# A forward 640-point transform in five full 128-row tables in place of four full ones and 32-row remainders

## The chip, the cores and the metric

The kernel runs on one core of one Trainium2 chip. Its time is device time in microseconds (us) of one execution. Before the change the median of three runs is 203.46 us (203.17 to 204.21). The core has TensorE (matmuls, PE in a profile, its weight loads PEld), VectorE (DVE), ScalarE (ACT), GpSimd (POOL) and SyncE (SP), which here issues all DMAs. Each engine works through its own instructions in order and waits on semaphores for the others.

## The reference

Two branches work on the layernormed input, `x` of 2048 rows and 640 columns, in bfloat16.

```
xn  = layernorm(x)                                   # over the 640 columns
s   = irfft2( rfft2(xn) * (w_r + i w_i) )            # 2048 x 321 spectrum
g   = silu( (gelu(xn @ w_gate) * (xn @ w_up)) @ w_down )   # 640 -> 1536 -> 640
out = x + s * g
```

So there is a feed-forward network (FFN), and beside it a two-dimensional Fourier transform, a product with a spectrum and the way back. The transform is made of matmuls with sine tables that the kernel builds itself.

## The kernel before, in words

The 2048 rows are split as 128 x 16: slab `n1` (0 to 15) holds the 128 rows with the remainder `n1`, and lies as a `[128, 640]` slice of `X`. The FFN runs in four groups `g` of four slabs: per group 24 halves (`ffn_half`: gate or up product of one tile of 128 of the 1536 features, five matmuls of 512 columns) and 12 thirds (`down_third`: eight matmuls of 320 columns each). A gate half ends in a gelu on ScalarE (`ge`), an up half in a product on VectorE (`uT`). Their PSUM banks `psg` and `psu` have two buffers each.

The spectral work is woven between the pieces of the FFN. The order of all engines is written out by hand: `back` is the list of FFN pieces, and `put(s, ...)` hangs an item behind piece `s`. Nothing reorders it afterwards. Pieces 16 to 23 are the last halves of FFN group 0, 24 to 35 its thirds, 36 to 59 the halves of group 1, 60 to 71 its thirds. Since every engine works in that order, an item whose input is late holds back what was put behind it on the same engine.

The forward transform of one slab has these steps:

- `stats`, `root`, `norm`: mean and variance on VectorE, the power -0.5 on GpSimd, the norm in place on VectorE (slabs 4 to 7 on ScalarE).
- `fold_a`, `fold_b`, for a pair of slabs on VectorE: sums and differences of the two halves of the 640 columns (`uvt`), then of mirrored columns. This uses the symmetry of cosines and sines and of even and odd frequencies, and leaves four blocks of 160 values. They are stored as four chunks of 128 and one chunk of 4 x 32.
- `slab_S1`: five matmuls, one per chunk, with the table `Tfwd` of the slab: the transform along the rows. ScalarE copies the result from PSUM (`pz`) to `Zt`, one of four places in `zbuf`.
- `group_D`, for one slab and then five groups of three (`DF`): the transform along the columns with the table `FT`. Each block of 160 is one matmul with 128 rows and one with 32 rows, both 161 columns wide, the second added to the first in PSUM (`d_group`). The two PSUM tiles `pd` are then copied, written to every other element of `zd`, and four DMAs per group bring `zd` to the DRAM scratch `ZDR`.

The PSUM pool `psB` has two buffers, which `pz`, the two `pd` tiles of a group and, outside this stage, other tiles take in turn. So the transform behind a group waits until the group's first `pd` tile has been copied out.

After the last group, `load_B2` reads `ZDR` back as `B`; it is the gate between the forward stage and the second row stage (`s2_in`, first matmuls `px`), the product with the spectrum, and the way back, which uses `d_group` with another table (`FI`). GpSimd also builds the tables `MG` (`mg_build`) and halves the edge columns of the weights (`w_edge`).

Of the kernel before, what the change touches and what calls it, by code (L numbers as in the profile page):

```python
# [14 lines left out]
P = 128  # L15
# [3 lines left out]
LP = 322  # L19
LH = 161  # L20
HD = 160
F = 1536
NT = F // P
NS = 16
# [52 lines left out]
def build(nc, env):  # L77
# [59 lines left out]

    Tinv = consts.tile([P, NS, P], BF16)
    Tfwd = consts.tile([P, NS, P], BF16)
    FT = consts.tile([P, 5, LH], BF16)  # L140
    FI = consts.tile([P, 5, LH], BF16)
    MG = consts.tile([P, 2, 2, 64], BF16)
    N1 = consts.tile([P, 2, P], BF16)
# [6 lines left out]
    def gtile(shape, dt):  # L150
        n = 1
        for k in shape:
            n *= k
        w = n if dt != BF16 else n // 2
        ap = GEN[:, goff[0]:goff[0] + w]
        goff[0] += w
        assert goff[0] <= NH * L // 2
        if dt != INT32:
            ap = ap.bitcast(dt)
        if len(shape) > 1:  # L160
            names = "abcdefg"[:len(shape)]
            ap = ap.rearrange("p (%s) -> p %s" % (" ".join(names), " ".join(names)), **dict(zip(names, shape)))
        return ap
# [58 lines left out]
    make_identity(nc, ident)  # L222
    lint = gtile([LH], INT32)
    nc.gpsimd.iota(lint, pattern=[[1, LH]], base=0, channel_multiplier=0)
    vt = gtile([NS, P], INT32)

    def vt_iota(h):
# [13 lines left out]
    def affine(name, src, a, b):  # L241
        t = c1(name)
        nc.vector.tensor_scalar(out=t, in0=src, scalar1=float(a), scalar2=float(b), op0=ALU.mult, op1=ALU.add)
        return t
# [19 lines left out]
    def times(name, src, k, by):  # L264
        t = c1(name)
        nc.vector.scalar_tensor_tensor(out=t, in0=src, scalar=k, in1=by, op0=ALU.mult, op1=ALU.mult)
        return t
# [8 lines left out]

    def fwd_consts():
        cq = affine("cq", h_f, -320.0, 320.0)
        a_m = affine("a_m", pf, 4.0, 130.0)
        b_2 = affine("b_2", pf, 2.0, 385.0)  # L280
        b_3 = affine("b_3", pf, 2.0, 65.0)
        a_r = affine("a_r", s_f, 4.0, 2.0)
        s21 = affine("s21", s_f, 2.0, 1.0)
        b_r = fma("b_r", times("hs", s21, 1.0, hi_f), 1.0, cq)
        kc.append(cq)
        ab.extend([(a_m, b_0), (a_m, b_1), (a_m, b_2), (a_m, b_3), (a_r, b_r)])

    def inv_consts():
        i_0 = affine("i_0", pf, 4.0, 0.0)
# [46 lines left out]
    ftm = gtile([5, LH], FP32)  # L336

    def ft_v(g):
        nc.scalar.activation(out=fv[:, g, :], in_=lint, func=ACT.Identity, scale=ab[g][0], bias=ab[g][1])

    def ft_phase(t, k):
        v = fv[:, 5 * t:5 * t + 5, :]
        if k == 0:
            nc.gpsimd.tensor_scalar(out=ftm, in0=v, scalar1=1.0 / 1280.0, scalar2=MAGIC, op0=ALU.mult, op1=ALU.add)
        elif k == 1:
            nc.gpsimd.tensor_scalar(out=ftm, in0=ftm, scalar1=MAGIC, scalar2=-1280.0, op0=ALU.subtract, op1=ALU.mult)
        else:
            nc.gpsimd.tensor_tensor(out=v, in0=v, in1=ftm, op=ALU.add)

    def ft_sin(t):  # L350
        nc.scalar.activation(out=(FT, FI)[t], in_=fv[:, 5 * t:5 * t + 5, :], func=ACT.Sin,
                             scale=TWO_PI / 1280.0 * (1.0 - 2e-7))

    mg = {}
# [86 lines left out]
        done.add(("n", n1))  # L441

    uvs = {}

    def fold_a(pair):
        xn = X[:, 2 * pair:2 * pair + 2, :]
        assert ("n", 2 * pair + 1) in done
        uvs[pair] = uvt = work.tile([P, 2, D], BF16, tag="uv", bufs=2, name="uvt")
        nc.vector.tensor_tensor(out=uvt[:, :, 0:320], in0=xn[:, :, 0:320], in1=xn[:, :, 320:640], op=ALU.add)
        nc.vector.tensor_tensor(out=uvt[:, :, 320:640], in0=xn[:, :, 0:320], in1=xn[:, :, 320:640], op=ALU.subtract)  # L450

    def fold_b(pair):
        xf[pair] = f = work.tile([P, 2, D], BF16, tag="xf", bufs=2, name="f")
        s4 = uvs.pop(pair).rearrange("p k (t d) -> p k t d", t=2)
        dm = f[:, :, 0:512].rearrange("p k (g d) -> p k g d", g=4)
        dr = f[:, :, 512:640].rearrange("p k (g d) -> p k g d", g=4)
        for gs, op in ((slice(0, 4, 3), ALU.add), (slice(1, 3), ALU.subtract)):
            nc.vector.tensor_tensor(out=dm[:, :, gs, :], in0=s4[:, :, :, 32:160], in1=s4[:, :, :, 287:159:-1], op=op)
            nc.vector.tensor_tensor(out=dr[:, :, gs, :], in0=s4[:, :, :, 0:32], in1=s4[:, :, :, 319:287:-1], op=op)

    def chunk(f, k, c):
        return f[:, k, c * P:(c + 1) * P]

    def slab_T(n1, eng):
        assert ("n", n1) in done
# [16 lines left out]
    zbuf = fv.rearrange("p g l -> p (g l)").bitcast(BF16)[:, 0:4 * D].rearrange("p (s c k) -> p s c k", s=4, c=5)  # L482

    def slab_S1(n1):
        f = xf[n1 // 2]
        pz = psB.tile([P, 5, P], FP32, tag="b")
        for c in range(5):
            nc.tensor.matmul(pz[:, c, :], lhsT=chunk(f, n1 % 2, c), rhs=Tfwd[:, n1, :], start=True, stop=True)  # L488
        Zt[n1] = zbuf[:, n1 % 4]
        nc.scalar.copy(out=Zt[n1], in_=pz)  # L490

# [13 lines left out]
    DF = [(0, 1)] + [(n0, 3) for n0 in range(1, NS, 3)]  # L505
    DG = [(n0, min(3, NS - n0)) for n0 in range(0, NS, 3)]

    def group_D(i):
        n0, n = DF[i]
        pd = d_group([Zt.pop(n0 + a) for a in range(n)], FT, LH)  # L510
        zd = work.tile([P, 3, 2, LP], BF16, tag="zd", bufs=2, name="zd")[:, 0:n]
        for b in range(2):
            ev = nc.vector.tensor_copy if i in (2, 5) and b == 1 else nc.scalar.copy
            ev(out=zd.rearrange("p a c (m b) -> p a c m b", b=2)[:, :, :, :, b], in_=pd[b])  # L514
        for a in range(2):
            if n == 1:
                nc.sync.dma_start(out=ZDR[a, :, n0].rearrange("c p l -> p c l"), in_=zd[a:P:2, 0, :, 0:L])
            else:
                for c in range(2):
                    nc.sync.dma_start(out=ZDR[a, c, n0:n0 + n].rearrange("n p l -> p n l"),  # L520
                                      in_=zd[a:P:2, :, c, 0:L])

    warm_bank = []

# [308 lines left out]
        put(17 + 2 * k, slab_T, 4 + k, 2)  # L833
    put(17, stats, 8)
    put(19, stats, 9)
    put(23, fold_a, 0)
    for it in ((silu_table,), (tinv_sin, 0), (tinv_sin, 1), (ft_sin, 0)):
        put(23, *it)
    put(24, fold_b, 0)
    put(28, mg_mask)  # L840
    put(25, root, 8, 2)
    put(25, fold_a, 1)
    for q in range(4):
        put(24 + q, tfwd, q)
    put(27, norm, 8)
    put(28, fold_b, 1)
    put(29, stats, 10)
    put(28, ft_sin, 1)
    put(29, mg_sin)
    put(29, mg_build)  # L850
    put(31, norm, 9)
    put(32, stats, 11)
    put(33, root, 10, 2)
    put(34, norm, 10)
    put(35, norm, 11)
    put(38, stats, 12)
    put(41, stats, 13)
    put(41, root, 12, 2)
    put(42, stats, 14)
    put(43, norm, 12)  # L860
    put(44, norm, 13)
    put(44, stats, 15)
    put(45, root, 14, 2)
    put(46, norm, 14)
    put(47, norm, 15)
    F0 = 30
    for i, (n0, n) in enumerate(DF):
        a = F0 if i == 0 else F0 + 5 * i - 3
        for k in range(n):
            put(a + k, slab_S1, n0 + k)  # L870
        put(a + n, group_D, i)
    for pair in range(6):
        b = F0 + 3 * pair + (0 if pair < 4 else 3)
        put(b, fold_a, pair + 2)
        put(b + 1, fold_b, pair + 2)
    z_end = F0 + 26
    for k in range(4):
        put(32 + 3 * k, slab_T, 8 + k, 2)
# [85 lines left out]
```

## Time and profile before

| what | value |
|---|---|
| median of the runs shown | 203.46 us (203.17 to 204.21) |
| the profiled execution | 203.13 us |
| its span, first to last instruction | 201.1 us |
| mean granted TensorE clock | 0.998 |
| TensorE busy, instructions | 194.5 us, 1558 |
| VectorE busy | 128.1 us |
| ScalarE busy | 122.6 us |
| GpSimd busy | 34.0 us |
| forward stage, first transform to the last group's end | 42.6 to 81.4 us |
| first `B` load issued, first `px` matmul | 88.19 us, 92.53 us |

A profile here has a page and answers from the trace. A line of the groups gives line of the kernel, engine, operation, output and inputs by the program's names, shape and count, and then busy us, mean ns of one, and the idle time of the engine before them with what ended it. A timeline line gives start, duration, engine, line and operation, and how many equal instructions are merged. Matmuls overlap and their ends are modelled, so TensorE is read by the distance between starts. The chain of work that ended last is followed back from the last instruction, step by step, to what released it.

### The profile page before, as it was taken

The numbers are of one execution on the slowest core, as the hardware profiler recorded it, in microseconds if no ns is written. First come the engines' busy times: TensorE is split into PE (matmuls) and PEld (weight loads), VectorE is DVE, ScalarE is ACT, GpSimd is POOL, SyncE is SP. The second block draws the span as 40 slices with busy tenths as digits, with TensorE's granted clock in tenths as the row PEclk, the third lists the DMA queues.
The fourth block names the chain that finished last, engine by engine and source line by source line (L and its number), as shares of the span: only waits on it lengthen the run. The fifth ranks groups of instructions, "written<-read, shape, count | busy, mean of one in ns | idle before, by whom it ended". The sixth has DMA issues, their size and how long they took to land.

```text
span 201.1 us, 4180 instructions
## 1 busy us (share of the span) xinstructions
PE 194.5 (97%) x1558; PEld 118.9 (59%) x1573; DVE 128.1 (64%) x339; ACT 122.6 (61%) x209; POOL 34.0 (17%) x61
## 2 busy tenths in 40 slices
PE   7899999999999999999999999999999999999993
PEld 5678854777555555576644333457775555556762
DVE  7786966677398972544566475333258777867672
ACT  2448657966886777414888778325475647476631
POOL 4327779972101100000000000000000000000000
PEclk9999999999999999999999999999999999999999
DMA  6999999656566675139944102379401444224312
GB/s 173 308 301 307 372 341 186 135 144 232 124 173 156 158 276 171 54 97 296 243 134 132 64 34 101 131 179 316 163 0 65 101 115 117 72 91 140 92 62 68
DMA packets 39444, 32.29 MB, mean 161 GB/s; under 512 B 14209, under 2 KB 37377, under 8 KB 39169
## 3 DMA queue, kind: packets, MB, share of 16 engines
q1 hardware_dynamic: 39424, 32.04, 55.9%
q8 instruction: 12, 0.20, 0.4%
q14 instruction: 8, 0.06, 0.1%
HBM read 19.03 MB, written 7.88 MB: 134 GB/s over the span
## 4 chain that ended last, share of the span: by engine, by line
PE 91%; DVE 5%; issue 1%; POOL 1%; ACT 0%
PE psu L727 25%; PE psg L727 25%; PE psg L751 13%; PE psu L751 12%; PE pd L498 5%; PE pz L488 2%; PE pv L644 2%; PE pu L592 2%; PE pd L502 2%; PE px L565 2%; DVE st L182 1%; POOL rst L198 1%; DVE X L204 1%; DVE mva L187 0%; DVE uT L733 0%
## 5 line engine op out<-in xcount | busy, mean ns | idle before, releaser
L727 PE MATMUL psu<-xnT,Wu 128*128 128x512 bf16 (+2 forms) x289 | 61.0, 339 | 0.7 <-issue 0.2
L727 PE MATMUL psg<-xnT,Wg 128*128 128x512 bf16 (+2 forms) x286 | 60.3, 338 | 1.0 <-issue 0.5
L733 DVE TENSOR_TENSOR uT<-psu,ge 128x512 bf16<-128x512 f32 (+2 forms) x59 | 34.3, 584 | 30.1 <-PE psu L727 22.5
L731 ACT ACTIVATE ge<-psg 128x512 bf16<-128x512 f32 (+2 forms) x59 | 30.5, 518 | 27.8 <-PE psg L727 25.9
L751 PEld LDWEIGHTS <-uT 128*128 128x128 bf16 x384 | 36.3, 98 | 14.7 <-issue 0.6
L727 PEld LDWEIGHTS <-Wu 128*128 128x128 bf16 x295 | 26.6, 98 | 23.0 <-issue 2.9
L727 PEld LDWEIGHTS <-Wg 128*128 128x128 bf16 x295 | 26.6, 98 | 21.9 <-issue 1.6
L751 PE MATMUL psg<-Wd,uT 128*128 128x320 bf16 (+1 forms) x192 | 30.2, 303 | 0.0
L751 PE MATMUL psu<-Wd,uT 128*128 128x320 bf16 (+1 forms) x192 | 29.2, 296 | 0.0
L577 DVE TENSOR_TENSOR X<-xs,W 128x972 bf16<-128x972 bf16 (+2 forms) x22 | 13.3, 648 | 10.2 <-ACT xs L573 10.2
L646 ACT CAST W<-pv 128x640 bf16<-128x640 f32 x16 | 11.1, 692 | 5.4 <-PE pv L644 5.4
L182 DVE BATCH_NORM_STATS2 st<-X 128x6 f32<-128x320 bf16 x32 | 14.2, 482 | 0.0
L514 ACT CAST zd<-pd 128x966 bf16<-128x966 f32 (+1 forms) x10 | 10.4, 1100 | 5.3 <-PE pd L502 5.3
L669 ACT ACTIVATE W<-pd 128x960 bf16<-128x960 f32 (+2 forms) x14 | 10.1, 780 | 5.0 <-PE pd L502 4.9
L490 ACT CAST GEN<-pz 128x640 bf16<-128x640 f32 x16 | 11.0, 696 | 3.2 <-PE pz L488 3.2
L598 ACT CAST X<-pu 128x486 bf16<-128x486 f32 (+4 forms) x22 | 12.3, 557 | 0.3
L573 ACT CAST xs<-px 128x972 bf16<-128x972 f32 (+2 forms) x11 | 10.3, 937 | 2.1 <-PE px L565 2.1
L198 POOL TENSOR_TENSOR rst<-ve,mhalf 128x1 f32<-128x1 f32 (+2 forms) x9 | 6.5, 717 | 26.6 <-DVE ve L196 26.6
L675 DVE TENSOR_TENSOR W<-W 128x960 bf16<-128x960 bf16 (+1 forms) x12 | 6.8, 600 | 4.8 <-ACT W L669 4.8
L702 DVE TENSOR_TENSOR Yall<-Yall,G 128x640 bf16<-128x640 bf16 (+3 forms) x18 | 8.1, 450 | 2.1 <-ACT G L756 1.9
L760 DVE SCALAR_TENSOR_TENSOR G<-th,psu 128x320 bf16<-128x320 f32 x8 | 3.9, 488 | 8.2 <-ACT th L759 8.2
L703 DVE TENSOR_TENSOR Yall<-Yall,xt 128x640 bf16<-128x640 bf16 (+3 forms) x18 | 8.2, 455 | 0.6
(138 smaller groups left out, 198.0 us busy)
## 6 DMA issues: line engine op xcount, KB each, us to landing
W<-W SPq DMA_DIRECT2D x4, 642.0 KB, 4.2
xt<-in_A_x_dram SPq DMA_DIRECT2D x8, 320.0 KB, 3.8
ZDR<-zd SPq DMA_DIRECT2D x20, 120.4 KB, 3.2
UDR<-X SPq DMA_DIRECT2D x10, 240.8 KB, 2.5
out_dram<-Yall SPq DMA_DIRECT2D x14, 160.0 KB, 2.1
B<-ZDR SPq DMA_DIRECT2D x8, 240.8 KB, 4.2
W<-UDR SPq DMA_DIRECT2D x4, 481.5 KB, 7.0
X<-in_A_x_dram SPq DMA_DIRECT2D x3, 640.0 KB, 7.1
```

What stands on the lines that cost most here:

```text
L182: nc.vector.bn_stats(out=st[:, k, :], in_=X[:, n1, 320 * k:320 * k + 320])
L490: nc.scalar.copy(out=Zt[n1], in_=pz)
L514: ev(out=zd.rearrange("p a c (m b) -> p a c m b", b=2)[:, :, :, :, b], in_=pd[b])
L573: nc.scalar.copy(out=xs, in_=px[:, :, 0:n * w].rearrange("p k (h l) -> p k h l", l=w))
L577: nc.vector.tensor_tensor(out=pp[-1], in0=xs, in1=WT[:, :, h0:h0 + n, l0:l0 + w], op=ALU.mult)
L598: nc.scalar.copy(out=us[:, :, :, c0:c0 + (w + 1 - m) // 2], in_=pv[:, :, :, m:w:2])
L646: nc.scalar.copy(out=vs, in_=pv)
L669: nc.scalar.activation(out=eo[:, b, :, a0:a1].rearrange("p k a n -> p a k n"), in_=py[b][:, a0:a1], func=ACT.Copy, scale=(2.0 if silu[a0] ...
L727: nc.tensor.matmul(ps, lhsT=WT[:, c, t * P:(t + 1) * P], rhs=xnT[g][:, c, c0:c1_], start=(c == 0), stop=(c == 4))
L731: nc.scalar.activation(out=ges[t], in_=ps, func=ACT.Gelu_apprx_tanh)
L733: nc.vector.tensor_tensor(out=uT[g][:, t, c0:c1_], in0=ps, in1=ges[t], op=ALU.mult)
L751: nc.tensor.matmul(ph, lhsT=uT[g][:, t, j * P:(j + 1) * P], rhs=Wd[:, t, c0:c1_], start=(t == 0), stop=(t == NT - 1))
```

## The change

The frequencies 0 to 320 are split into those divisible by five and the others.

- For the first, only the sum of the five blocks of 128 columns matters. `fold_y` forms it for a pair of slabs in three additions (512, 256 and 256 elements); it is the fifth chunk, 128 values. Pairs 0 and 1 have it on VectorE, pairs 2 to 7 on GpSimd.
- For the others, adding the same block to all five blocks changes nothing, so `fold_x` subtracts one block from the others (two instructions, 768 and 256 elements). `fold_a` and `fold_b` then work on the four blocks left, with two additions or subtractions of 512 elements each, and give four chunks of 128.
- The table `FT` has five parts of 128 columns; sample points are moved by half a step, so that the columns that are always zero need no entry. They are set once by a memset in `zds`, two fixed buffers in place of the pool's.
- `group_D` does five matmuls of 128 rows and 128 columns per slab. The four first chunks go to four PSUM banks, and the fifth to the free end of these banks. The copies to `zd` are one of all groups' 768 elements, two of 384, one of 256 and one of 128; the elements go to strides of two in runs of four or two, and of five. In groups 1 and 5 the second bank pair's copies are VectorE's, before it was in groups 2 and 5.
- The plan of statistics, norms and folds is written anew. Statistics 14 and 15, their norms and the fold of the last pair lie three to four pieces later than before, and `mg_build` eight pieces later.

```diff
-    FT = consts.tile([P, 5, LH], BF16)
+    FT = consts.tile([P, 5, P], BF16)
+    zds = [consts.tile([P, 3, ZW], BF16, name=f"zd{k}") for k in range(2)]
+    for k in range(2):
+        nc.gpsimd.memset(zds[k][:, :, 325:326], 0.0)
...
+    def fold_y(pair, eng):
+        xn = pair_x(pair)
+        y0s[pair] = y = work.tile([P, 2, P], BF16, tag="y0", bufs=3, name="y0")
+        t = ytbuf
+        for out, i0, i1 in ((t, xn[:, :, 0:256], xn[:, :, 256:512]), (y, t[:, :, 0:P], t[:, :, P:256]),
+                            (y, y, xn[:, :, 512:640])):
+            eng.tensor_tensor(out=out, in0=i0, in1=i1, op=ALU.add)
+
+    def fold_x(pair):
+        xn = pair_x(pair)
+        xps[pair] = xp = xpbuf
...
+        ref = blocks(xn)[:, :, 2:8:5, :]
+        nc.vector.tensor_tensor(out=outer(xp), in0=outer(xn),
+                                in1=ref.unsqueeze(1).to_broadcast([P, 3, 2, 2, 64]), op=ALU.subtract)
+        nc.vector.tensor_tensor(out=blocks(xp)[:, :, 6:2:-3, :], in0=blocks(xn)[:, :, 6:2:-3, :], in1=ref,
+                                op=ALU.subtract)
...
     def fold_a(pair):
...
-        nc.vector.tensor_tensor(out=uvt[:, :, 0:320], in0=xn[:, :, 0:320], in1=xn[:, :, 320:640], op=ALU.add)
-        nc.vector.tensor_tensor(out=uvt[:, :, 320:640], in0=xn[:, :, 0:320], in1=xn[:, :, 320:640], op=ALU.subtract)
+        lo, hi = (xp[:, :, o:o + 384].rearrange("p s (t e) -> p s t e", e=192)[:, :, :, 0:P] for o in (0, 320))
+        for k, op in enumerate((ALU.add, ALU.subtract)):
+            nc.vector.tensor_tensor(out=uvt[:, :, 256 * k:256 * k + 256].rearrange("p s (t e) -> p s t e", e=P),
+                                    in0=lo, in1=hi, op=op)
...
     def fold_b(pair):
...
         for gs, op in ((slice(0, 4, 3), ALU.add), (slice(1, 3), ALU.subtract)):
-            nc.vector.tensor_tensor(out=dm[:, :, gs, :], in0=s4[:, :, :, 32:160], in1=s4[:, :, :, 287:159:-1], op=op)
-            nc.vector.tensor_tensor(out=dr[:, :, gs, :], in0=s4[:, :, :, 0:32], in1=s4[:, :, :, 319:287:-1], op=op)
+            nc.vector.tensor_tensor(out=dm[:, :, gs, :], in0=s4[:, :, :, 0:P], in1=s4[:, :, :, 255:127:-1], op=op)
...
+    BY_DVE = (1, 5)
...
     def group_D(i):
         n0, n = DF[i]
-        pd = d_group([Zt.pop(n0 + a) for a in range(n)], FT, LH)
...
+        ps = [psB.tile([P, 2, 512], FP32, tag="b", name=f"pd{b}") for b in range(2)]
+        for a in range(n):
+            z = Zt.pop(n0 + a)
+            for g in range(5):
+                o = ps[g // 2][:, g % 2, a * P:a * P + P] if g < 4 else ps[a // 2][:, a % 2, 384:512]
+                nc.tensor.matmul(o, lhsT=z[:, g, :], rhs=FT[:, g, :], start=True, stop=True)
...
+        ev[0](out=zq[:, :, :, :, 2:10:2], in_=src[0].rearrange("p a c (q r) -> p a c q r", r=4))
+        for h in range(2):
+            ev[1](out=zq[:, :, :, :, 1 + 6 * h:4 + 6 * h:2],
+                  in_=src[1][:, :, :, 64 * h:64 * h + 64].rearrange("p a c (q i) -> p a c q i", i=2))
+        for b in range((n + 1) // 2):
+            m = min(2, n - 2 * b)
+            ev[b](out=y_cols(zd, 2 * b, m), in_=ps[b][:, 0:m, 384:512].rearrange("p a (c m) -> p a c m", c=2))
...
+            (40, (stats, 13), (root, 12, 2)), (41, (fold_a, 4)),
+            (42, (fold_b, 4), (norm, 12)), (43, (norm, 13), (half_stats, 14, 0), (fold_y, 6, gp)),
+            (44, (fold_x, 5), (half_stats, 14, 1)), (45, (fold_a, 5)), (46, (fold_b, 5), (fold_x, 6)),
+            (47, (fold_a, 6)), (48, (fold_b, 6), (half_stats, 15, 0)), (49, (half_stats, 15, 1), (root, 14, 2)),
+            (50, (norm, 14), (norm, 15), (fold_y, 7, gp)), (51, (fold_x, 7)), (52, (fold_a, 7), (fold_b, 7))):
```

## The prediction

> **What bounds the kernel now.** I read the page's busy shares, then the chain that ended last, then the groups by form, and last the timelines of the engines around the forward 640-point stage (42 to 82 us).
>
> ```profile
> span 201.1 us, 4180 instructions
> ...
> PE 194.5 (97%) x1558; PEld 118.9 (59%) x1573; DVE 128.1 (64%) x339; ACT 122.6 (61%) x209; POOL 34.0 (17%) x61
> ...
> PE 91%; DVE 5%; issue 1%; POOL 1%; ACT 0%
> ```
>
> TensorE carries 91% of the chain and idles 6.6 us in all. So a us of matmul removed is a us gained, unless another engine makes TensorE wait; every edit is judged by that. The granted clock is 0.998, with nothing to gain there. The profiled execution took 203.13 us (span 201.1, 2.0 outside), 0.33 below the median of 203.46.
>
> The stage's matmuls, from TensorE's timeline (start, us, line, count):
>
> ```profile
> 49.71 1.02 PE L498 MATMUL pd<-FT,GEN 128*128 128x161 bf16 x12
> 50.67 0.39 PE L502 MATMUL pd<-FT,GEN 32*128 32x161 bf16 x12
> 50.99 0.39 PE L727 MATMUL psg<-xnT,Wg 128*128 128x512 bf16 x1
> ...
> 60.97 0.44 PE L488 MATMUL pz<-Tfwd,f 128*128 128x128 bf16 x5
> 61.25 0.38 PE L727 MATMUL psu<-xnT,Wu 128*128 128x512 bf16 x1
> ```
>
> Ends are modelled, so starts count: a group of three slabs holds TensorE from 49.71 to 50.99, 1.28 us; five 128x128x128 matmuls, each with weights of its own, 0.28 us, or 56 ns each.
>
> Groups by form (busy us, mean ns of one) give the other prices; VectorE's eviction of 966 elements stands there with 1240 ns:
>
> ```profile
> L514 ACT CAST zd<-pd 128x966 bf16<-128x966 f32 x8 | 9.5, 1245 | 4.8 <-PE pd L502 4.8
> ...
> L458 DVE TENSOR_TENSOR f<-uvt 128x512 bf16<-128x512 bf16 x16 | 6.7, 421 | 2.0 <-PE pz L488 2.0
> ...
> L348 POOL TENSOR_TENSOR GEN<-GEN 128x805 f32<-128x805 f32 x2 | 3.2, 1612 | 0.2
> ...
> L514 ACT CAST zd<-pd 128x322 bf16<-128x322 f32 x2 | 0.9, 521 | 0.5 <-PE pd L502 0.5
> ```
>
> **TensorE.** A full group becomes 15 matmuls of the 56 ns kind, 0.84 us for 1.28: 5 x 0.44 = 2.2. The first group (4 + 4 matmuls, 43.95 to 44.51, 0.56) becomes five, 0.28. Group 2 also waited 0.19 between its second and third matmul (57.41 to 57.67, 0.07 elsewhere) for a Z copy on ScalarE; the new order needs that slab later. Together -2.67. The Trainium skill, "TensorE: Matmul & The Clock Gate", section "Back-to-back issue gap", speaks against this: it gives about 81 ns for a weight load plus a 128-column matmul in a real stream. By it a group would cost an estimated 1.2 us and the stage would gain about 0.7. The 0.28 us row contradicts it here, so I take 56 ns.
>
> **Evictions.** Both ScalarE rows write every other element: two of 966 take 2.35 us, two of 322 take 0.90, so 1.13 ns per element plus 0.02, and a 0.12 tail. Groups 2, 3, 4 are now emptied by ScalarE alone, in order 768 (first bank pair), 384, 384 (second), 256 (first), 128 (second): 0.89 + 0.45 + 0.45 + 0.31 + 0.12 = 2.2 us until the first PSUM buffer is free, 1.24 before. Behind the group stand two FFN halves (2 x 1.08); then the next column transform wants that buffer. With 0.1 to start and 0.1 to pass the semaphore it waits 0.2. Bounds: nothing (the first copy may start three matmuls early), and 0.9 each if runs of two and four elements cost 30% more than the rows. Groups 1 and 5 give the second bank pair to VectorE (2 x 0.52 + 0.32); ScalarE is then done in 1.3.
> Behind ScalarE's evictions queues the gelu of the next half, and behind that VectorE's uT product.
>
> **VectorE.** A pair cost 2 x 0.41 + 2 x 0.33 + 2 x 0.14 = 1.76 start to start, and costs 0.47 + 0.20 (differences, 768 and 256 elements on the 512 and 640 rows' slope) + 4 x 0.33 = 2.0, plus 0.09 where one waits for the other. The broadcast block is new; if it ran at half speed, +0.5 per pair. The block sums of pairs 0 and 1 add 0.33 + 0.2 + 0.2 each at 39 and 43 us, where nothing is due at once. VectorE idles 16 of 45 us between 35 and 80 and hides all this, except at the last pair, where the plan has moved statistics, norms and folds three to four slots later. The old fold ended at 74.1 for a transform at 77.4; 3.3 us of cover are spent.
>
> That stretch, counted from the end of group 3's matmuls. TensorE: halves 46 to 53 (8 x 1.08), transforms 10 to 13 (4 x 0.28), group 4 (0.84): it wants slab 14 after 10.6 us. VectorE: evictions 2.4, gelu 0.6, semaphores: uT of half 47 starts at 3.1. Then uT 0.58, fold 6 0.8 + 0.7, statistics 15 0.4, uT 0.58, statistics and aggregate 0.8, ve to root to norm 1.1 (48.20 to 49.35 in the trace), two norms 0.74, uT 0.58, fold 7 0.8 + 0.8 + 0.7: 11.7. TensorE waits 1.1 us in this stretch; the buffer waits of groups 3 and 4 lie inside it. Bounds: 0.6 (evictions faster) to 2.
>
> **GpSimd.** Six block sums move there, 512 + 256 + 256 elements. By 1612 ns for 805: 1.0 + 0.5 + 0.5, with fixed parts and gaps 2.3 us. Beside VectorE's folds GpSimd is slower:
>
> ```profile
> 37.95 0.92 POOL L360 TENSOR_SCALAR vg<-kr,n1x,phm 128x16 int32<-128x16 int32 x1
> 38.84 0.36 POOL L360 TENSOR_SCALAR vg<-kr,n1x,phs 128x16 int32<-128x16 int32 x1
> ...
> 51.26 0.95 POOL L135 TENSOR_SCALAR W<-W 128x64 bf16<-128x64 bf16 x1 [1.95 <-DMA W<-W]
> ...
> 79.17 0.46 POOL L135 TENSOR_SCALAR W<-W 128x64 bf16<-128x64 bf16 x1 [9.92 <-DMA ZDR<-zd]
> ```
>
> The 0.92 and the 0.95 lie beside VectorE tensor-tensor work (to 38.7, and 51.0 to 51.9): half speed or less, while VectorE's own folds there keep their 0.42 and 0.48. For pair 7 the sum starts after norm 15, together with uT (0.58), then fold 7 (2.1 us of contested time). At half speed 0.7 of its 2.3 remain when the fold is done: transform 14 waits 0.65 longer. Bounds: 0 (no contention) and 1.8 (no progress beside folds). Queued behind the sums on GpSimd: mg_build (3.3 us, 42.5 to 45.8 in the trace, now after pair 5's sum), then root 12, which VectorE's norm 12 needs at about 61. By the rows root 12 is done at 60 to 61; at half speed this just holds.
> On this the Trainium skill, "SBUF — State Buffer", section "Who interferes with whom", says more: a VectorE instruction with two SBUF inputs and a GpSimd one that reads SBUF exclude each other, and whoever comes second waits in full. By it VectorE's folds too would wait for block sums; the rows show only GpSimd paying, with instructions of 0.36 us.
>
> **Last step.** Group 5's eviction goes to the DMA queue: first B load issued at 88.19, 4.2 to land in the DMA view's median, first px matmul at 92.53: TensorE has no slack there. So 0.1 more for group 5's eviction (1.35 for 1.24) is paid. Nothing after px changes. The first group's output goes in four DMAs instead of two, 1.3 us more on SP's queue at 47; behind them SP waits 1.6 us (51.9 to 53.5) for group 1's copies, which takes it up. W's edge (now behind root 12) and mg_build are wanted at 94 and 85.7, over 20 us later: nothing. Tables, two memsets and two iotas at the start: VectorE does three small steps fewer, GpSimd 0.7 us more, while it idled 1.58 for VectorE; the first statistics wait for x, landed at 3.08. Nothing.
>
> **Sum.** -2.67 + 0.2 (group 2) + 1.1 (stretch) + 0.65 (block sum 7) + 0.1 = -0.6. Against its own execution 202.5; against the median 202.8 to 202.9. I take 202.8.
>
> **Rivals.**
> *Full gain.* GpSimd is not slowed, evictions run at the short rows' cost: -2.67 + 0.6 to 1.4, so 201.4 to 202.2, about 201.8. For it: VectorE's idle time. Against: the contested rows.
> *Block sums block.* The same contention, harder: GpSimd makes almost no progress beside folds, or folds wait for its 1 us instructions. Then pair 5's sum, mg_build and root 12 come 1 to 2 us late, norm 12 holds the fold of pair 5 and transform 10 waits 1 to 2; and transform 14 waits 1.2 more than I have: +1 to +3, about 205.0. It decides from the point where a sum of 2.3 us takes over 3.9. For it: 0.92 against 0.36; the last sum has no cover. The skill's exclusion rule above is this rival.
> *Evictions by short runs.* ScalarE pays 30% more: a wait of 0.9 at group 2 (+0.7), and 0.8 more in the stretch, whose eviction and later uT grow alike: +0.9, 204.4. For it: writing every other element already costs 1245 ns where 972 packed elements cost 966.
> *Little gain on TensorE.* The new stream keeps the 72 ns spacing of the 161-column matmuls (49.71 to 50.50 for twelve): 15 x 72 = 1.08, a group gains 0.2, the stage 1.4; less the same 2.05 lost: +0.65, 204.1. The 56 ns row speaks against it. The skill's 81 ns would be this rival; by it the time would be an estimated 204.8.
>
> **Numbers.** Forecast (-0.2 to -1.2) 0.42; full gain 0.25; block sums 0.22; evictions 0.07; little gain 0.04. 0.5% (1.0 us) is about what a measurement tells from no change. Faster: all of full gain but a little, and a third of the forecast: 0.36. Slower: most of the block sums and some of the last two: 0.25. Same: 0.39. The range goes from the full gain's end, less 0.2 of scatter, to the middle of the block sums' dearer half: 201.2 to 205.4. The forecast's own: 202.2 to 203.3.
>
> **What would show it.** TensorE: 15 matmuls in 0.84 us from the first one of a group to the next line's. Waits of transforms 7, 10, 13 on ScalarE's y copies near 0.2; of transform 14 over 0.5 on GpSimd's sum or VectorE's fold 7. GpSimd instructions of 512 elements of 1.0 us where VectorE is quiet and up to 2 beside folds. First px about 0.6 earlier than 92.53. I am wrong if transform 10 waits too, if VectorE's folds are longer than 0.5, or if transform 14 does not wait at all.

## The result and the profile after

The changed kernel is slower: 213.06 us median (212.06 to 214.35) against 203.31 us for the kernel before, measured beside it (203.1 to 204.21), six runs each. The ratio is 1.048, with a 95% interval of 1.0451 to 1.0509. The forecast was 202.8 us, and the range ended at 205.4.

The page of the changed kernel: span, busy shares, and the chain by engine.

```profile
span 211.0 us, 4153 instructions
...
PE 196.3 (93%) x1525; PEld 118.8 (56%) x1525; DVE 142.3 (67%) x346; ACT 130.8 (62%) x223; POOL 49.8 (24%) x83
...
PE 63%; DVE 9%; ACT 5%; POOL 2%; issue 2%; DVEq 0%
```

TensorE carried 91% of the chain before; now it is 63%. Nearly the whole loss lies in the forward stage. The matmuls of its first group start at 44.69 us (43.95 before), those of its last group end at 90.79 (81.44 before, a modelled end). From there to the first `px` matmul it is 11.1 us in both profiles (101.9 and 92.53). TensorE before, at the two ends of that stretch:

```profile
43.95 0.45 PE L498 MATMUL pd<-FT,GEN 128*128 128x161 bf16 x4
...
81.05 0.39 PE L502 MATMUL pd<-FT,GEN 32*128 32x161 bf16 x12
```

TensorE's timeline of the changed kernel (start, us, line, count; in brackets the idle time before and who ended it) shows the gain of the change and what eats it:

```profile
44.69 0.44 PE L567 MATMUL pd<-FT,GEN 128*128 128x128 bf16 x5 [0.41 <-ACT GEN L537]
...
50.56 1.00 PE L567 MATMUL pd<-FT,GEN 128*128 128x128 bf16 x15
51.39 1.24 PE L792 MATMUL psg<-xnT,Wg 128*128 128x512 bf16 x5
...
58.02 0.61 PE L535 MATMUL pz<-Tfwd,f 128*128 128x128 bf16 x4 [2.95 <-DVE zd L578]
...
58.53 2.34 PE L792 MATMUL psu<-xnT,Wu 128*128 128x512 bf16 x5
...
67.33 0.38 PE L535 MATMUL pz<-Tfwd,f 128*128 128x128 bf16 x4 [1.86 <-ACT zd L578]
...
76.42 0.38 PE L535 MATMUL pz<-Tfwd,f 128*128 128x128 bf16 x4 [1.86 <-ACT zd L578]
...
85.74 0.38 PE L535 MATMUL pz<-Tfwd,f 128*128 128x128 bf16 x4 [1.86 <-ACT zd L578]
...
90.79 1.24 PE L792 MATMUL psg<-xnT,Wg 128*128 128x512 bf16 x5
```

A group takes from 50.56 to 51.39, 0.84 us, as forecast. But transform 5 waits 2.95 us for VectorE's copies of group 1, and transforms 7, 10 and 13 wait 1.86 each for ScalarE's copies of groups 2, 3 and 4: 8.5 us together. The half behind transform 5 takes 2.13 us to the next start, where others take 1.08. The windows show why (start and end; length; busy us of PE, PEld, VectorE, ScalarE and GpSimd, each with its instructions; granted clock; DMA share; GB/s):

```profile
50.00:58.00 8.00, 5.07 (x41) 2.87 (x38) 7.90 (x11) 5.74 (x8) 6.81 (x8) 0.99 0.60 148
58.00:63.00 5.00, 4.98 (x33) 3.02 (x34) 4.93 (x12) 1.88 (x3) 3.83 (x11) 0.67 0.49 133
```

After the idle stretch the granted clock is 0.67 over 5 us, which loses 5.0 x 0.33 = 1.65 us. From the first group's start to the last group's end the stage takes 46.10 us against 37.49: +8.61, of the 9.9 us by which the span grew. The known parts are 8.53 (the four waits) + 1.65 (clock) - 2.48 (matmuls: 0.28 and 5 x 0.44) = 7.7; the remaining 0.9 is not broken down here.

ScalarE's timeline behind group 2, whose matmuls end at 63.15:

```profile
63.18 1.23 ACT L572 CAST zd<-pd 128x768 bf16<-128x768 f32 x1
64.24 2.32 ACT L574 CAST zd<-pd 128x384 bf16<-128x384 f32 x2
66.22 1.42 ACT L578 CAST zd<-pd 128x256 bf16<-128x256 f32 x2
```

The 768 elements take 1.06 us to the next start, but each of the two copies of 384 takes 0.99 on average as well. The first PSUM buffer, which the 768 and the 256 must both leave, is free 4.1 us after the group (the 256 end at 67.28), not 2.2.

VectorE's timeline ahead of the wait of transform 5, and then GpSimd's beside it:

```profile
49.25 0.76 DVE L499 TENSOR_TENSOR uvt<-GEN 128x512 bf16<-128x512 bf16 x2
50.12 1.72 DVE L507 TENSOR_TENSOR f<-uvt 128x512 bf16<-128x512 bf16 x2
51.76 1.55 DVE L208 TENSOR_SCALAR X<-X,mva,rst 128x640 bf16<-128x640 bf16 x2
53.23 1.50 DVE L489 TENSOR_TENSOR GEN<-X 128x768 bf16<-128x768 bf16 x1
...
55.33 2.27 DVE L574 CAST zd<-pd 128x384 bf16<-128x384 f32 x2
```

```profile
50.22 1.34 POOL L476 TENSOR_TENSOR GEN<-X 128x512 bf16<-128x512 bf16 x1
...
53.08 1.24 POOL L476 TENSOR_TENSOR GEN<-X 128x512 bf16<-128x512 bf16 x1
```

Two folds of 512 take 0.76 us where GpSimd computes no sum (at 49.25; it has only the small power of `root` there) and 1.72 beside a sum; the differences of 768 elements, 0.55 with no sum beside them (36.03 us in the same trace), take 1.50. Group 1's matmuls are done at 51.4, but its copies stand behind these instructions in VectorE's queue and start at 55.33. The two of 384 then take 1.02 us each (55.33 to 57.37) where I had 0.52.

So two suspects: copies that cost more than their elements, and GpSimd's additions, which hold VectorE up.

### The profile page after: what moved, and what is told of

Its sections match the earlier page's. It is cut to its first block, busy times and chain, and to the rows that moved or that the text cites. A ratio compares the mean times of both kernels' runs of the same rounds, so it can differ in the third digit from the quotient of the medians.

```text
span 211.0 us, 4153 instructions
## 1 busy us (share of the span) xinstructions
PE 196.3 (93%) x1525; PEld 118.8 (56%) x1525; DVE 142.3 (67%) x346; ACT 130.8 (62%) x223; POOL 49.8 (24%) x83
## 4 chain that ended last, share of the span: by engine, by line
PE 63%; DVE 9%; ACT 5%; POOL 2%; issue 2%; DVEq 0%
PE psu L792 17%; PE psg L792 16%; PE psg L816 10%; PE psu L816 9%; ACT zd L574 3%; PE pd L545 2%; PE pv L709 2%; PE pu L657 2%; PE px L630 2%; PE pz L535 2%; DVE f L507 1%; PE pd L567 1%; POOL vg L376 1%; ACT zd L578 1%; DVE GEN L489 1%
## 5 line engine op out<-in xcount | busy, mean ns | idle before, releaser
L792 PE MATMUL psu<-xnT,Wu 128*128 128x512 bf16 (+2 forms) x295 | 62.6, 344 | 0.5 <-DVE uT L798 0.3
L792 PE MATMUL psg<-xnT,Wg 128*128 128x512 bf16 (+2 forms) x295 | 61.4, 340 | 0.0
L796 ACT ACTIVATE ge<-psg 128x512 bf16<-128x512 f32 (+2 forms) x59 | 31.1, 528 | 26.7 <-PE psg L792 24.9
L535 PE MATMUL pz<-Tfwd,f 128*128 128x128 bf16 x64 | 7.0, 230 | 8.8 <-ACT zd L578 5.6
L711 ACT CAST W<-pv 128x640 bf16<-128x640 f32 x16 | 11.1, 692 | 5.4 <-PE pv L709 5.4
L535 PEld LDWEIGHTS <-f 128*128 128x128 bf16 x64 | 5.1, 103 | 13.6 <-issue 5.0
```

The costliest lines, as they stand in the source:

```text
L535: nc.tensor.matmul(pz[:, c, :], lhsT=chunk(n1 // 2, n1 % 2, c), rhs=Tfwd[:, n1, :], start=True, stop=True)
L711: nc.scalar.copy(out=vs, in_=pv)
L792: nc.tensor.matmul(ps, lhsT=WT[:, c, t * P:(t + 1) * P], rhs=xnT[g][:, c, c0:c1_], start=(c == 0), stop=(c == 4))
L796: nc.scalar.activation(out=ges[t], in_=ps, func=ACT.Gelu_apprx_tanh)
```

## Experiments

### The two suspects singly and together

Packed copies: same elements, same engines, same order, but written side by side, so the spectrum lies in the wrong order and the output is not the reference's. (The zero column that a memset sets moves behind them; the diff leaves that out.)

```diff
...
-        ev[0](out=zq[:, :, :, :, 2:10:2], in_=src[0].rearrange("p a c (q r) -> p a c q r", r=4))
+        ev[0](out=zd[:, :, 5:261].rearrange("p a (c x) -> p a c x", c=2), in_=src[0])
         for h in range(2):
-            ev[1](out=zq[:, :, :, :, 1 + 6 * h:4 + 6 * h:2],
-                  in_=src[1][:, :, :, 64 * h:64 * h + 64].rearrange("p a c (q i) -> p a c q i", i=2))
+            ev[1](out=zd[:, :, 261 + 128 * h:389 + 128 * h].rearrange("p a (c x) -> p a c x", c=2),
+                  in_=src[1][:, :, :, 64 * h:64 * h + 64])
...
-            ev[b](out=y_cols(zd, 2 * b, m), in_=ps[b][:, 0:m, 384:512].rearrange("p a (c m) -> p a c m", c=2))
+            ev[b](out=zd[:, 2 * b:2 * b + m, 517:645], in_=ps[b][:, 0:m, 384:512])
```

> The changed kernel, but the copies from PSUM to zd write their elements packed (the same number of instructions and elements, reads unchanged, zd in another order, so the spectrum is in the wrong order). Theory A, the scattered writes are the main cost: a copy of 384 elements goes from 1.16 us to about 0.5 on ScalarE, the first pd buffer of groups 2 to 4 is free 2.2 us after the group and not 4.0, the three waits of 1.86 us of transforms 7, 10 and 13 go to 0.3 or less (-5.2), VectorE's copies of group 1 are 1.2 us shorter in all: 206 us (205 to 207). Theory B, the contention of GpSimd's block sums with VectorE's folds is the main cost and ScalarE only waits for others: 211 us or more.

Measured: 208.25 us, ratio 1.0257 (1.0236 to 1.0278). ScalarE's timeline behind group 2 of this kernel:

```profile
61.73 0.81 ACT L571 CAST zd<-pd 128x768 bf16<-128x768 f32 x1
62.57 0.87 ACT L573 CAST zd<-pd 128x384 bf16<-128x384 f32 x2
63.31 0.56 ACT L577 CAST zd<-pd 128x256 bf16<-128x256 f32 x2
```

The same elements are out in 2.1 us (61.73 to 63.87) instead of 4.5 (63.18 to 67.64), and the three waits of 1.86 are gone. The time fell between the two expectations: TensorE now waits on VectorE, as the waits of this kernel say (total us, times, longest):

```profile
PE pz L535 <- DVE f L507: 2.6, 2, 1.7
PE pz L535 <- DVE zd L577: 1.9, 1, 1.9
```

No block sums on GpSimd: pairs 2 to 7 use the sum of pair 1, so their frequencies divisible by five are wrong; the copies are those of the changed kernel.

```diff
     def fold_y(pair, eng):
         xn = pair_x(pair)
+        if pair > 1:
+            y0s[pair] = y0s[1]
+            return
```

> The changed kernel without the block sums of pairs 2 to 7 on GpSimd; the fifth chunk of pair 1 stands in for theirs, so the frequencies divisible by five are wrong. Copies as in the changed kernel. Theory A: VectorE's folds of 50 to 55 us return from 0.86 and 1.50 us to 0.42 and 0.55, VectorE reaches the copies of group 1 when the group ends (about 51.4, not 55.3), transform 5 no longer waits 3.1 us and TensorE's clock no longer falls after it (1.5 us): 208.5 us (207.5 to 209.5); the waits of 1.86 us stay. Theory B: 205 us or less.

Measured: 207.83 us, ratio 1.0236 (1.0216 to 1.0257). The groups of VectorE between 44 and 92 us, and TensorE's waits:

```profile
L510 DVE TENSOR_TENSOR f<-uvt 128x512 bf16<-128x512 bf16 x13 | 5.0, 424 | 0.3
```

```profile
PE pz L538 <- ACT zd L581: 5.6, 3, 1.9
```

The folds have their short times again (424 ns on average against 534, and 548 against 989 for the differences of 768 elements). Transform 5 does not wait, the granted clock is 1.00 from 44 to 92 us, and the three waits of 1.86 on ScalarE stay, as theory A expected.

Both edits in one kernel:

```diff
+        if pair > 1:
+            y0s[pair] = y0s[1]
+            return
...
+        ev[0](out=zd[:, :, 5:261].rearrange("p a (c x) -> p a c x", c=2), in_=src[0])
...
+            ev[1](out=zd[:, :, 261 + 128 * h:389 + 128 * h].rearrange("p a (c x) -> p a c x", c=2),
+                  in_=src[1][:, :, :, 64 * h:64 * h + 64])
...
+            ev[b](out=zd[:, 2 * b:2 * b + m, 517:645], in_=ps[b][:, 0:m, 384:512])
```

> The two edits together: packed copies, and no block sums of pairs 2 to 7 on GpSimd (spectrum in the wrong order, frequencies divisible by five wrong). If the two causes are all there is, the shorter matmuls show: 201.3 to 202.5 us, about 1.5 below the kernel before, with no wait of TensorE over 0.6 us in the stage. If something else costs, it stays above 203.5.

Measured: 201.91 us, ratio 0.9943 (0.9926 to 0.9959). Singly the edits take 4.8 and 5.2 us from 213.06, together 11.15, which is more than the loss of 9.75. So the two account for all of the loss, and what is left is a gain of 1.1 us against the kernel before, measured beside it (203.03). In this profile the stage takes 35.38 us from the first group's start to the last group's end, 2.11 less than before; the matmuls alone promise 2.48. But the first group starts 1.35 us later there (45.30 for 43.95), 0.38 of it a wait for its Z copy; the rest is not broken down.

### Does TensorE wait for the sums, or for VectorE?

In one more kernel the copies are packed, GpSimd computes every sum where it did, and nobody reads it (here and in the next diff the lines of the packed copies are left out):

```diff
-        y0s[pair] = y = work.tile([P, 2, P], BF16, tag="y0", bufs=3, name="y0")
+        y = work.tile([P, 2, P], BF16, tag="y0" if pair < 2 else "y1", bufs=2 if pair < 2 else 1, name="y0")
+        y0s[pair] = y if pair < 2 else y0s[1]
```

> Packed copies, and GpSimd computes the sums of pairs 2 to 7 in their old places, but nobody reads them: the column transforms of those pairs take the sum of pair 1 (part of the output is left wrong by that, and by the packed copies). Theory A (VectorE's folds are shut out while GpSimd adds, and come late): folds and differences beside sums stay at 0.8 us and more each, and the time is that of the kernel with packed copies, 208 us (206.5 to 208.5). Theory B (the transforms wait for GpSimd's slow results): without a reader the loss goes, 201.9 us (201.3 to 202.7), as with no sums at all.

In a second, each of these additions is replaced by two memsets of the same tile:

```diff
-            eng.tensor_tensor(out=out, in0=i0, in1=i1, op=ALU.add)
+            if pair < 2:
+                eng.tensor_tensor(out=out, in0=i0, in1=i1, op=ALU.add)
+            else:
+                eng.memset(out, 0.0)
+                eng.memset(out, 0.0)
```

> As the kernel with packed copies and unused sums, but each of GpSimd's additions for pairs 2 to 7 is replaced by two memsets of the same tile, which read nothing from SBUF. The sums are left out. Theory A (two engines that read SBUF with two inputs shut each other out; a GpSimd instruction that reads nothing does not): folds at 0.28 to 0.42 us each as without GpSimd, 201.9 us (201.3 to 202.7). Theory B (any instruction of GpSimd that touches SBUF shuts VectorE out): folds beside memsets are longer than 0.6, and the time is over 203.5.

Measured: 207.86 us with unused sums, ratio 1.0228 (1.0212 to 1.0243), against 208.25 with sums that are used; 202.67 us with memsets, ratio 0.9972 (0.9958 to 0.9987). VectorE with unused sums (timeline), then VectorE and GpSimd with memsets (groups, 44 to 92 us):

```profile
50.04 1.72 DVE L508 TENSOR_TENSOR f<-uvt 128x512 bf16<-128x512 bf16 x2
```

```profile
L512 DVE TENSOR_TENSOR f<-uvt 128x512 bf16<-128x512 bf16 x13 | 5.0, 422 | 0.3
```

```profile
L481 POOL MEMSET GEN<- 128x512 bf16 x6 | 3.2, 535 | 0.3
```

Almost nothing depends on when the sums are ready. What costs is that VectorE's own instructions take two to three times as long while GpSimd adds. With 14.4 us of memsets in GpSimd's queue (24 of 256 and 12 of 512 elements) the folds and differences do not, and the time is 0.8 us above the kernel with nothing in their place. Theory A held in both kernels. So it is not GpSimd's activity as such that holds the folds; it is something that the additions have and the memsets lack.

That this is the reading alone is not shown, and two rows speak for caution. The norms of VectorE are longer beside memsets too: 604 ns on average, against 432 in the kernel with packed copies and no sums, and 540 in the changed kernel (first line below, 44 to 92 us). And a GpSimd instruction with one tensor input, in the kernel without sums, was itself held, 1.05 us where its like take 0.30, while VectorE's differences beside it kept their 0.55 and 0.28 (the other lines).

```profile
L208 DVE TENSOR_SCALAR X<-X,mva,rst 128x640 bf16<-128x640 bf16 x7 | 4.1, 604 | 0.8 <-POOL rst L202 0.8
```

```profile
50.35 1.05 POOL L376 TENSOR_SCALAR MG<-sg,z 128x32 bf16<-128x32 f32 x1
...
50.48 0.55 DVE L492 TENSOR_TENSOR GEN<-X 128x768 bf16<-128x768 bf16 x1
50.95 0.28 DVE L494 TENSOR_TENSOR GEN<-X 128x256 bf16<-128x256 bf16 x1
```

### The two prices by themselves

Bare instructions were put behind the end of the kernel before: copies of 384 f32 of PSUM to bf16 of SBUF, each three times on each engine, with every step-th element written, or runs of r every other element, one run per 10; then additions of 512 on VectorE alone (6), on GpSimd alone (4), on both at once (12 and 6), and copies on VectorE (12) beside additions on GpSimd (6).

```diff
...
+    for copy in (nc.scalar.copy, nc.vector.tensor_copy):
+        for o, i in cases():
+            for _ in range(3):
+                copy(out=o, in_=i)
...
+    for k in range(6):
+        nc.gpsimd.tensor_tensor(out=block(10 + k % 2), in0=block(7), in1=block(5), op=ALU.add)
+    for k in range(12):
+        nc.vector.tensor_tensor(out=block(12 + k % 2), in0=block(0), in1=block(1), op=ALU.add)
+    for k in range(6):
+        nc.gpsimd.tensor_tensor(out=block(10 + k % 2), in0=block(12), in1=block(5), op=ALU.add)
+    for k in range(12):
+        nc.vector.tensor_copy(out=block(14 + k % 2), in_=block(1))
```

> The kernel before, with a row of bare instructions behind its end: copies of 384 elements from PSUM on ScalarE and VectorE, packed and with steps of 2, 5, 8, 16 and 26 elements and in runs of two and four of every ten; then 512-element additions on VectorE and GpSimd alone and together, then VectorE copies beside GpSimd. Theory A1, a scattered write costs by the stretch it covers (about 0.27 ns per byte, from 1.0 us for 3840 bytes): step 5 takes 1.2 us, step 16 3.5 us, step 26 5.5 us, runs of two 1.2 us, runs of four 0.7 us. Theory A2, it costs by the number of jumps (about 2.7 ns each for an element that has no neighbour): step 5, 16 and 26 all take 1.2 us. Together, a VectorE addition (0.42 alone) and a GpSimd one (1.2 alone): if each waits for the other, VectorE's are 1 us and more; if only GpSimd pays, VectorE's stay at 0.42. VectorE copies do not change beside GpSimd.

| 384 elements, written | bytes covered | ScalarE, us | VectorE, us |
|---|---|---|---|
| packed | 768 | 0.478 | 0.558 |
| every 2nd element | 1536 | 0.585 | 0.585 |
| runs of 4 per 10 | 1920 | 0.690 | 0.691 |
| runs of 2 per 10 | 3840 | 1.219 | 1.219 |
| every 5th | 3840 | 1.219 | 1.219 |
| every 8th | 6144 | 1.855 | 1.853 |
| every 16th | 12288 | 1.758 | 1.758 |
| every 26th | 19968 | 1.85 | 1.85 |

From step 2 up to step 8 (16 bytes) the price goes with the bytes covered, about 0.28 ns for each (1.27 us more for 4608 bytes more): two patterns that cover 3840 bytes cost the same 1.219 us, though one has runs and the other none. From 16 bytes on it no longer grows: 1.76 to 1.86 us, about 4.7 ns per element (estimate, 1.8 / 384). Of the expectations on record, the price by the stretch holds up to 16 bytes and fails beyond (1.76 and 1.85 us for 3.5 and 5.5). The other, 1.2 us for every gap, fails too. The two engines pay alike from the second row on. The Trainium skill, "SBUF — State Buffer", section "Door 1: The DMA port swizzle", says that SBUF has lines of 16 bytes and that bf16 may be stepped by 8 for free. The place of the bend agrees with the 16 bytes; the "for free" does not: step 8 costs 3.9 times the packed copy on ScalarE.

The additions, from the timelines of VectorE and GpSimd (first alone, then together, then GpSimd beside VectorE's copies):

```profile
263.24 2.10 DVE L964 TENSOR_TENSOR room<-room 128x512 bf16<-128x512 bf16 x6
...
270.41 9.83 DVE L971 TENSOR_TENSOR room<-room 128x512 bf16<-128x512 bf16 x12
280.17 2.50 DVE L975 COPY room<-room 128x512 bf16<-128x512 bf16 x12
```

```profile
265.57 4.47 POOL L966 TENSOR_TENSOR room<-room 128x512 bf16<-128x512 bf16 x4 [186.23 <-DVE room L964]
270.11 7.83 POOL L969 TENSOR_TENSOR room<-room 128x512 bf16<-128x512 bf16 x6
280.05 9.16 POOL L973 TENSOR_TENSOR room<-room 128x512 bf16<-128x512 bf16 x6 [2.10 <-DVE room L971]
```

Alone, an addition of 512 starts every 0.34 us on VectorE (0.415 long) and every 1.11 on GpSimd (1.148 long). Together each starts every 1.29 us on both engines: they take turns, and each instruction of VectorE waits for a whole one of GpSimd's. The six VectorE additions that overlap take 1.365 each, the six after them 0.410.

### Copies in another order

Only the order changes: the first PSUM buffer's two copies go first.

```diff
         ev[0](out=zq[:, :, :, :, 2:10:2], in_=src[0].rearrange("p a c (q r) -> p a c q r", r=4))
+        m = min(2, n)
+        ev[0](out=y_cols(zd, 0, m), in_=ps[0][:, 0:m, 384:512].rearrange("p a (c m) -> p a c m", c=2))
         for h in range(2):
...
-        for b in range((n + 1) // 2):
-            m = min(2, n - 2 * b)
-            ev[b](out=y_cols(zd, 2 * b, m), in_=ps[b][:, 0:m, 384:512].rearrange("p a (c m) -> p a c m", c=2))
+        if n == 3:
+            ev[1](out=y_cols(zd, 2, 1), in_=ps[1][:, 0:1, 384:512].rearrange("p a (c m) -> p a c m", c=2))
```

> Only the order of a group's copies changes: 768 elements, then the first bank pair's y copy of 256, then the second pair's 384, 384 and 128. Theory A (the wait is the release of the first PSUM buffer, 4.0 us after the group): it is now free after about 1.06 + 0.72 = 1.8 us, under the two halves (2.2 us) before transforms 7, 10 and 13, and their waits of 1.86 fall under 0.2. The second buffer is still free only at 4.0 and is wanted at about 3.5 by transforms 8, 11 and 14: up to 0.5 each comes back. Gain 3 x 1.2 to 1.7 = 3.6 to 5: 209 us (208 to 210). Theory B (what counts is ScalarE's whole time in the copies, 4.0 us per group, with the gelus and Z copies queued behind it): the wait moves whole to the next transform, and the time stays at 211.5 or more. The late folds beside GpSimd's sums stay in both.

Measured: 211.29 us (210.54 to 211.71), ratio 1.0401 (1.0375 to 1.0428). Two of TensorE's waits in its timeline (transform 5 still waits, 3.29 us):

```profile
67.78 0.38 PE L535 MATMUL pz<-Tfwd,f 128*128 128x128 bf16 x4 [0.88 <-ACT zd L579]
...
86.05 0.68 PE L535 MATMUL pz<-Tfwd,f 128*128 128x128 bf16 x4 [1.71 <-DVE f L507]
```

Theory A was right on the cause, since the three waits of 1.86 on ScalarE shrink to one of 0.88, and wrong on the gain, 1.8 us instead of 3.6 to 5; the time comes out close to theory B's 211.5. While TensorE stood still for ScalarE, VectorE had caught up; without that pause three transforms wait for late folds, 2.8 us in all.

### The sums on VectorE

```diff
-    ve, gp = nc.vector, nc.gpsimd
+    ve = gp = nc.vector
```

> Only the engine of the block sums of pairs 2 to 7 changes: VectorE does them, in the same places. Nothing is left out. Theory A (two engines shut each other out; the sum as such is cheap): six sums of about 0.33 + 0.2 + 0.2 = 0.75 us on VectorE, folds back to 0.28 to 0.42 each, GpSimd's mg_build and root steps early; the time is that of the kernel without sums (207.8) plus what of 4.5 us has no cover: 208.5 us (207.8 to 209.8), with the three waits of 1.86 on ScalarE's copies still there, and no wait of over 1 us at transform 5. Theory B (the sums themselves are too much work wherever they stand): 211 us or more, with waits on VectorE's folds.

Measured: 210.17 us, ratio 1.0345 (1.0329 to 1.036), between the two expectations; the waits of 1.86 stay (5.6 us in 3), transform 5 waits 1.8 us. The same with packed copies:

> Packed copies, and VectorE does the sums of pairs 2 to 7, which are used. The copies leave the spectrum in another order, so the output is not the reference's. Theory A (VectorE has become the bound of the stage, with hardly an idle us between 44 and 76): six sums of 0.75 us are 4.5 us, of which as with the scattered copies about half is not covered: 201.9 + 2.3 = 204.2 us (203.2 to 205.5), with waits of transforms on folds. Theory B (VectorE has room; the other kernels with sums on VectorE lost their time to copies): 202.5 us or less.

Measured: 206.12 us, ratio 1.0143 (1.0128 to 1.0159), so 4.2 us above the kernel with packed copies and no sums. The window from 44 to 76 us of that kernel, with the columns as above:

```profile
44.00:76.00 32.00, 29.51 (x239) 17.71 (x238) 30.09 (x87) 22.93 (x44) 6.38 (x13) 1.00 0.72 196
```

VectorE is busy 30.1 of 32 us (24.6 in the kernel before) and has taken over as the bound. A sum costs it 0.97 us to the next start (65.71 to 66.68), not 0.75: its three additions depend on each other, and each starts only when the one before has ended. Six are 5.8 us, of which only 1.6 were covered. Both expectations missed: theory A was right on the cause, too low on the amount.

### Towards a kernel that computes everything

Order and engine together, and then the second bank pair in natural order of frequency, so that it is copied in one pass of 744 elements (runs of four) and two of 12:

```diff
-    nc.gpsimd.iota(meo[:, 1].rearrange("p (h q i) -> p h q i", h=2, i=2), pattern=[[3, 2], [5, 32], [1, 2]], base=0,
+    nc.gpsimd.iota(meo[:, 1].rearrange("p (q h i) -> p q h i", h=2, i=2), pattern=[[5, 32], [3, 2], [1, 2]], base=0,
...
+        ze = zd[:, :, 5:645].rearrange("p a (c x) -> p a c x", c=2)
+        zo = zd[:, :, 10:650].rearrange("p a (c q e) -> p a c q e", c=2, e=10)
+        ev[1](out=zo[:, :, :, 0:31, 2:10:2], in_=src[1][:, :, :, 2:126].rearrange("p a c (q r) -> p a c q r", r=4))
+        ev[1](out=ze[:, :, :, 1:5:2], in_=src[1][:, :, :, 0:2])
+        ev[1](out=ze[:, :, :, 317:320:2], in_=src[1][:, :, :, 126:128])
```

> Both: the copies in the order 768, 256, 384, 384, 128, and the sums on VectorE. Nothing is left out. If the two causes are independent of how they are taken away, what is left of the 1.86 waits is at most 0.5 at transforms 8, 11 and 14, and VectorE carries 4.5 us of sums: 203.5 us (202.5 to 205). If VectorE is now the bound of the stage (sums, and 2.3 us of copies in groups 1 and 5), it shows as waits on folds and a time over 205.

> As the kernel with order and sums on VectorE, and the second bank pair's table in natural order of frequency, so that its two passes of 384 elements become one of 744 in runs of four, and two of 12 elements at the ends. If a copy costs by the stretch it covers (3840 bytes, about 1.0 us per pass, whatever it holds), the second pair takes about 1.05 + 2 x 0.2 = 1.45 instead of 2.0, the second buffer is free at about 3.5 and its waits go: 0.5 to 1 us faster than the kernel with two passes, 202.8 us (202 to 204). If it costs by the element, one pass of 744 takes the 2.0 us of the two and the time is that of the other kernel within 0.3.

Measured: 209.06 us, ratio 1.0311 (1.0279 to 1.0344), and 207.28 us, ratio 1.0212 (1.0197 to 1.0227). ScalarE with one pass:

```profile
61.26 1.38 ACT L577 CAST zd<-pd 128x744 bf16<-128x744 f32 x1
```

744 elements in one pass take 1.21 us to the next start (62.47); 768 in two take 2.0 in the changed kernel. That is near the price by bytes covered (1.05 was expected) and far from the price by elements. The step from two passes to one gains 1.8 us, more than expected. Both kernels are 4.5 to 5.6 us above my figures: VectorE is the bound here too, the case that was put at over 205, and TensorE waits for folds 2.9 to 3.2 us in three places in each. The fastest kernel that computes everything takes 207.28 us. With packed copies VectorE's sums alone put the time at 206.12, so neither GpSimd nor VectorE has room for the block sums in this order of work. Other places for them, and sums on TensorE or ScalarE, were not tried.

## Why the prediction was wrong, step by step

- **TensorE, -2.67: right.** 15 matmuls in 0.84 us, and with both causes gone the stage is 2.11 us shorter. The 56 ns held; the rival of little gain falls. Group 2's wait of 0.19 us is gone as forecast. But the first group now waits 0.41 us for its Z copy, which stands on ScalarE behind a table step (`sg`) that waited 1.3 us for VectorE; no term of the sum had this.
- **Evictions, "1.13 ns per element", "2.2 us until the first PSUM buffer is free", wait 0.2: wrong.** Both rows that I drew the slope from write every other element, so the slope was one per 4 bytes covered. The new copies write fewer elements over the same stretch. 768 elements took 1.06 us for 0.89, each 384 took 0.99 for 0.45, and the 256 took 1.06 (66.22 to 67.28) for 0.43 with the tail; the sum is 4.1 us, the wait 1.86 for 0.2, and it returns behind groups 2, 3 and 4 in full. I wrote that the waits of groups 3 and 4 lie inside the stretch's loss; they did not, there were three. The rival of short runs had the place; its 30% was 120% on the copies of 384.
- **VectorE and GpSimd, "VectorE's own folds there keep their 0.42 and 0.48": wrong for the block sums.** The rows were read rightly, but they are GpSimd instructions of 0.36 to 0.46 us with one tensor input. The new ones have two inputs and 1.2 us, and VectorE's folds wait for them. VectorE also had less idle time to hide this than I wrote: 13.5 us between 35 and 80, not 16. So the cost was not 0.65 us at transform 14, from a late sum, but late folds along the whole stage: taking the sums away gains 5.2 us. The rule of the Trainium skill that I gave 0.22 as a rival ("SBUF — State Buffer", "Who interferes with whom") agrees with the additions in the runs, with 1.29 us per pair. Its clause that a GpSimd instruction that only writes does not contend with a VectorE instruction of two SBUF inputs agrees with the folds beside memsets.
- **Groups 1 and 5 on VectorE: priced, but not placed.** I gave their copies 1.36 us and no queue. In the trace they stand behind 3.9 us of delayed folds and norms (51.4 to 55.33), and transform 5 waits 2.95 us, the longest wait of all. The clock loss of 1.65 us that follows was in none of my cases.
- **The stretch before the last pair, +1.1, and block sum 7: not seen.** Transform 14 hardly waits (it follows the half at 86.02 with 1.08 us). VectorE ended the last fold 15.0 us after group 3 (72.24 to 87.23), not 11.7, but TensorE had lost 1.86 us each to transforms 10 and 13. Where packed copies take those two waits away, the wait comes to light: transform 14 waits 1.70 us for the fold (timeline below, kernel with packed copies), where 1.1 + 0.65 was on record. Without the sums too, 0.34 us are left. So the size was about right, by luck: 1.36 of the 1.70 go with the sums, for which I had 0.65.

```profile
82.34 0.68 PE L535 MATMUL pz<-Tfwd,f 128*128 128x128 bf16 x4 [1.70 <-DVE f L507]
```

- **Last step, +0.1: not seen.** From the last group to `px` nothing changed.
- **The rival "block sums block"** had the mechanism of one of the two causes and the direction. It stopped at 205 to 206 because I let it act at transforms 10 and 14 only.

## What to carry to other kernels

A copy that writes bf16 with gaps was priced here by the stretch it covers, up to 16 bytes per element; so merge interleaved passes over one stretch into one, and take a slope only from rows with the same gap. Work moved to GpSimd is not free for VectorE when both read two SBUF tensors: a VectorE instruction can then take as long as GpSimd's, and everything queued behind it is late. And one wait hides the next: the copies in another order paid 1.8 us of the 3.6 to 5 expected, because late folds stood behind them; removing one of the two causes paid about 5 us, removing both 11.

## Not expected of the hardware

- VectorE's bf16 copies are not slowed by GpSimd's additions (0.278 us each throughout), but hold them: the GpSimd addition that began at 280.05 us ended only at 283.67, 1.0 us after the last of twelve copies; those after it took 1.14 each. This agrees with the Trainium skill, "SBUF — State Buffer", section "Who interferes with whom", by which such a copy takes the shared ports for itself.
- The clock: after idle waits of 2.95 and 3.29 us TensorE ran at half speed (a half of five matmuls in 2.13 us; the window after the first has 0.67). After 1.91 and 1.92 us, in the kernels with packed copies, it did not (1.00 from 56 to 62 us), and not after 2.16 us in the kernel with order and sums on VectorE (1.00 from 56.7 to 61 us). Where between 2.16 and 2.95 us it turns was not tried. The Trainium skill, "TensorE: Matmul & The Clock Gate", section "What's actually happening", gives an idle window of about 3.4 us. Here somewhat less was enough.
- Norms on VectorE (`X<-X,mva,rst`) also doubled beside the sums, 1.55 us for two against 0.80 without, though they read one tensor from SBUF, and they are longer beside memsets (604 ns against 432, above). What causes it was not tried.
